# One attention step in another order: products with v behind the scores, and a third of the transposes behind these

## The chip, the cores and the metric

The kernel runs on one core of a Trainium2 chip, as one program. The metric is the device time of one execution in microseconds (us), the median of several. The engines are named as in the profile: PE is TensorE (matmuls and transposes; PEld is its weight load), DVE is VectorE, ACT is ScalarE, POOL is GpSimd, and SP is the engine that issues most DMAs. Each engine works through its own instructions in the order in which the program has them.

## The reference

Three blocks follow each other: attention with a learned position bias, a dense feed-forward block, and an expert block in which each token goes to one of 8 experts. Only the order inside the attention changes.

```
B, H, S, D = 4, 8, 576, 64                              # batch, heads, sequence, head size
scores = q @ k.T / sqrt(D) + bias[head]                 # bias: a small MLP over log distances
attn   = exp(scores - max) / sum                        # softmax over the 576 keys
x      = (attn @ v), heads side by side                 # 2304 tokens x 512
h = x @ w_in ; x = (h - tanh(h)) @ w_out                # dense block, 512 -> 2048 -> 512
out = gate * (relu(x @ w1[e]) @ w2[e]), e = argmax(x @ w_gate)   # 8 experts
```

All arrays are float32.

## The kernel before

The attention is cut into 16 units. A unit is one batch entry and a pair of heads, and it has five steps, one for each block of query rows: blocks 0 to 3 have 128 rows for each of the two heads, and block 4 has the last 64 rows of both heads in one tile. The loop in `emit` (line 431) runs over x = 5 times the unit plus the step and issues what the row of `STEPS` (line 423) for this step names, one after the other. Nothing sorts the instructions afterwards, so this table is the order on every engine. One entry stands for these instructions:

- S0 and S1: the scores of a block and the first half of the softmax. S0 issues the 12 matmuls for both heads (`scores`, line 235; q and k are split in a high and a low part, so three products for each half of the keys; the two heads lie in the two halves of the array's 128 rows). The softmax on DVE (line 267) adds the bias and takes the maximum, once in S0 and once in S1. The scores lie in the two PSUM tiles of the tag `s`.
- E0 and E1: the exponentials on ACT (line 280) of the block of the step before. For block 4, POOL makes a copy (line 284).
- X0, X1 and X2: the transposes of p, the result of the exponentials, two steps later (`p_transposes`, line 311): nine 128 x 128 transposes in three groups of three, each group into one PSUM tile of the tag `xt`, of which there are three. DVE copies the group of X0 out (line 330), ACT the others (line 332). Block 4 has four transposes in X0 (line 335, copied out by ACT in lines 337 and 338) and one in X1 (line 342, copied out in lines 343 and 344).
- V, with a half and a block of keys: products of v with the transposed p (`pv`, line 346), two matmuls for the two heads, in the two halves of the array's columns. Half 0 covers the query blocks 0 and 1 (256 columns), half 1 the blocks 2 to 4 (320 columns). V-03 belongs to the unit before, V00 to this one. After the last block ACT copies the sum out (line 369).
- T and U: transposes of k, of q, or of the last 64 rows of both (`t`), for one or two units ahead (`transposes`, line 193), also into an `xt` tile; ACT copies them out as the high part (line 208). L and M: the low part on DVE (`lows`, line 224, lines 228 and 230), which reads the same PSUM tile once more. Lt ends with a copy on POOL (line 233).
- qk, v, bias, store, store_r: DMA loads and stores on SP. sums and spread: the reciprocals of the softmax sums, and their transpose (line 299).
- `*`: work for the next block that is spread over the attention steps: `Convert.step(x)` (line 499), a conversion of one weight tile every 2.4 steps, in stages: load, then two steps later a scaling on ACT (line 520), a clamp on POOL (line 525), bit operations on DVE (lines 531 to 538), a store; some tiles are split on ACT and DVE instead (lines 639 and 640). Tile i begins at x = 3 + 12 i / 5, rounded down, and is scaled two steps later.

A tile of a tag is given out again in the order in which the program has finished issuing the reads of the tiles before. The next matmul into it waits for the last of these reads. The dense block follows on PE as soon as the attention's instructions have been issued, in the same queues.

Of the kernel before, what the change touches and what calls it, by code (L numbers as in the profile page):

```python
# [127 lines left out]
class Attention:  # L128
# [246 lines left out]
    def begin(self, g):  # L375

        calls = {
            "qk": self.load_qk, "v": self.load_v,
            "bias": lambda i: self.load_bias(0, i),
        }  # L380
        for x, op, i in self.BESIDE:
            if x == g:
                if op in calls:
                    calls[op](i)
                elif op in ("k", "q", "t"):
                    self.transposes(i, op)
                    self.lows(i, op)
                else:
                    self.op(0, i, op)
# [30 lines left out]
    DONE = 3  # L420


    STEPS = (
# [5 lines left out]
    )  # L429

    def emit(self, extra):
# [3 lines left out]
        for x in range(self.DONE, 5 * nu + 5):  # L435
            for op in self.STEPS[x % 5]:
                if op == "*":
# [4 lines left out]
    def op(self, u, i, op):  # L442

        nu = len(self.units)
        x = 5 * u + i
        kind, w = op[0], int(op[-1]) if op[-1].isdigit() else None
        if kind == "S" and u < nu and (i < 4 or w == 0):
            if w == 0:
                self.scores(u, i)
            self.softmax1(u, i, w)  # L450
        elif kind == "E" and 0 <= x - 1 < 5 * nu and ((x - 1) % 5 < 4 or w == 0):
            self.softmax2((x - 1) // 5, (x - 1) % 5, w)
        elif kind == "X" and 0 <= x - 2 < 5 * nu and ((x - 2) % 5 < 4 or w < 2):
            self.p_transposes((x - 2) // 5, (x - 2) % 5, w)
        elif kind in "TU" and u + (1 if kind == "T" else 2) < nu:
            self.transposes(u + (1 if kind == "T" else 2), op[1])
        elif kind in "LM" and u + (1 if kind == "L" else 2) < nu:
            self.lows(u + (1 if kind == "L" else 2), op[1])
        elif kind == "V":
            v = u - 1 if op[1] == "-" else u  # L460
            if 0 <= v < nu:
                self.pv(v, int(op[-2]), (w,))
        elif op in ("sums", "spread", "store", "store_r"):
            if u > 0:
                getattr(self, op)(u - 1)
        elif op == "v":
            if 0 < u < nu - 1:
                self.load_v(u + 1)
        elif op == "qk" and 0 < u < nu - 2:
            self.load_qk(u + 2)  # L470
        elif op == "bias" and u + 1 < nu and self.units[u + 1][0] != self.units[u][0]:
            self.load_bias(self.units[u + 1][0], i)
# [956 lines left out]
```

## Time and profile before

| | us |
|---|---|
| median of 3 runs (lowest, highest) | 1058.62 (1055.51, 1059.51) |
| the profiled execution | 1059.38 |
| its span, first to last instruction | 1057.7 |
| busy in the span: PE, DVE, ACT, POOL | 1012.8, 762.7, 673.0, 186.8 |

The span has four stretches. The bias is made until about 79 us, attention runs until about 375 us, the dense block until about 800 us, and the experts to the end. The steps of the attention that PE runs back to back last from about 106 us on. A PE row of the timeline gives the start of the first matmul of a group and the end of its last; ends are modelled and overlap the next start, so distances between starts are what can be trusted.

### The profile page before, as it was taken

To read this page: it belongs to the slowest core of one execution; us is meant where nothing else is said; L and a number is where in the kernel's file an instruction comes from. 1 tells how busy PE (TensorE), PEld (TensorE's weight loads), DVE (VectorE), ACT (ScalarE), POOL (GpSimd) and SP (SyncE) were. 2 spreads that over 40 slices of the span, in tenths; PEclk is the share of its full clock that TensorE was granted. 3 is DMA by queue.
4 is the path that set the end of the run, shared out by engine and by line. 5 is a ranking of instruction groups with operands and counts; after the bars stand their busy time and mean duration, and the time that the engine had idled before them with its cause. 6 is when DMAs were issued, how large, how long until landed. Compare 5 with 4: busy or idle time off the path is not lost. (4 is left out here: it accounts for less than half of the span.)

```text
span 1057.7 us, 20501 instructions
## 1 busy us (share of the span) xinstructions
PE 1012.8 (96%) x7370; PEld 833.1 (79%) x7370; DVE 762.7 (72%) x1749; ACT 673.0 (64%) x1507; POOL 186.8 (18%) x224
## 2 busy tenths in 40 slices
PE   6788999999999999999999999999999999999994
PEld 3345666666666679889989889898899999999992
DVE  7874788888888789988899889888894544434210
ACT  7775888888878889765665665656883333333211
POOL 1100222222322411010110201202012131222111
PEclk9888999999999999999999999999999999999998
DMA  5747585685674443020200200203124244437200
GB/s 161 233 176 197 139 233 138 151 224 153 175 198 129 152 152 121 1 91 1 67 24 1 91 1 1 90 1 85 53 79 112 86 111 123 124 109 232 76 24 25
DMA packets 113750, 114.67 MB, mean 108 GB/s; under 512 B 67883, under 2 KB 82603, under 8 KB 113644
## 3 DMA queue, kind: packets, MB, share of 16 engines
q1 hardware_dynamic: 109628, 103.26, 34.0%
q0 software_dynamic: 3872, 9.72, 3.1%
q8 instruction: 60, 0.98, 0.4%
q14 instruction: 46, 0.38, 0.1%
q10 hardware_dynamic: 144, 0.33, 0.1%
HBM read 82.36 MB, written 31.18 MB: 107 GB/s over the span
## 5 line engine op out<-in xcount | busy, mean ns | idle before, releaser
L679 PE MATMUL h<-xh,w 128*128 128x384 f32 x768 | 215.4, 341 | 2.2 <-DVE t L698 2.2
L723 PE MATMUL y<-w,gh 128*128 128x512 f32 x576 | 179.4, 393 | 0.0
L679 PEld LDWEIGHTS h<-xh,w 128*128 128x128 f32 x768 | 140.6, 188 | 7.4 <-DVE t L698 3.5
L267 DVE CUSTOM_DVE_ANT_0 p<-s,bias 128x576 f32<-128x576 f32 x144 | 103.7, 753 | 36.7 <-PE s L247 18.8
L679 PE MATMUL h<-xl,w 128*128 128x384 f32 x384 | 129.2, 336 | 0.0
L723 PEld LDWEIGHTS y<-w,gh 128*128 128x128 f32 x576 | 106.6, 188 | 16.0
L1110 PE MATMUL eh<-xh,ew 128*128 128x288 f32 x512 | 117.6, 305 | 0.0
L723 PE MATMUL y<-w,gl 128*128 128x512 f32 x288 | 112.7, 391 | 0.2 <-DVE gl L710 0.2
L1132 PE MATMUL ey<-ehh,ew 128*128 128x288 f32 x512 | 112.7, 296 | 0.0
L280 ACT ACTIVATE p<-p,nm 128x576 f32<-128x576 f32 x144 | 110.7, 771 | 2.2 <-DVE nm L267 2.1
L1120 DVE SCALAR_TENSOR_TENSOR ehl<-eh,ehh 128x288 fp32r<-128x288 f32 x64 | 29.2, 457 | 110.5 <-ACT ehh L1119 101.6
L1119 ACT ACTIVATE ehh<-eh 128x288 fp32r<-128x288 f32 x64 | 26.3, 410 | 125.6 <-PE ey L1132 122.3
L691 ACT ACTIVATE z<-h 128x384 f32<-128x384 f32 x96 | 46.5, 484 | 77.1 <-PE h L679 77.1
L326 PE MATMUL px<-ident,p 128*128 128x128 f32 x576 | 92.8, 285 | 0.1
L358 PE MATMUL pv<-pt,vt 128*64 128x256 f32 (+1 forms) x256 | 87.2, 434 | 2.2 <-ACT pt L337 2.2
L326 PEld LDWEIGHTS px<-ident,p 128*128 128x128 f32 x576 | 63.3, 142 | 31.3 <-ACT p L280 11.1
L359 PE MATMUL pv<-pt,vt 128*64 128x256 f32 (+1 forms) x256 | 87.2, 434 | 0.0
L1110 PEld LDWEIGHTS eh<-xh,ew 128*128 128x128 f32 x512 | 86.6, 190 | 0.3 <-issue 0.2
L1132 PEld LDWEIGHTS ey<-ehh,ew 128*128 128x128 f32 x512 | 85.7, 188 | 0.0
L1110 PE MATMUL eh<-xl,ew 128*128 128x288 f32 x256 | 76.1, 297 | 0.0
L1132 PE MATMUL ey<-ehl,ew 128*128 128x288 f32 x256 | 75.6, 295 | 0.0
L332 ACT ACTIVATE pt<-px 128x384 f32<-128x384 f32 x128 | 60.9, 488 | 20.4 <-PE px L326 19.9
(474 smaller groups left out, 2202.0 us busy)
## 6 DMA issues: line engine op xcount, KB each, us to landing
rw<-in_moe_w SPq DMA_DIRECT2D x64, 256.0 KB
bias_d<-bo SPq DMA_DIRECT2D x36, 320.0 KB
bias<-bias_d SPq DMA_DIRECT2D x16, 576.0 KB
w<-in_moe_w_in SPq DMA_DIRECT2D x16, 512.0 KB
w<-in_moe_w_out SPq DMA_DIRECT2D x16, 512.0 KB
xt_d<-x SPq DMA_DIRECT2D x16, 288.0 KB
w_d<-wc SPq DMA_DIRECT2D x18, 256.0 KB
xf<-xt_d SPq DMA_DIRECT2D x24, 192.0 KB
```

The lines of the kernel that those rows point to most:

```text
L267: nc.vector.tensor_tensor_reduce(st["p"][:, c].rearrange("p (a x) -> p a x", a=2), st["ps", w][:, :, 0:288], bias[:, c].rearrange("p (a x) ...
L280: nc.scalar.activation(p[:, c], p[:, c], AF.Exp, bias=nm[:, w : w + 1], scale=-1.0, accum_out=self.st[u, "sm"][:, x : x + 1])
L326: nc.tensor.transpose(ps[:, 128 * j : 128 * j + 128], p[:, 128 * n : 128 * n + 128], self.ident)
L332: nc.scalar.activation(dst, src, AF.Copy)
L358: nc.tensor.matmul(ps[a, 0:n], v[:, j, :], pt[:, j, 0:n], start=j == 0, stop=False)
L359: nc.tensor.matmul(ps[z, 0:n], v[:, 6 + j, :], pt[:, 5 + j, 0:n], start=j == 0, stop=False)
L679: nc.tensor.matmul(ps[:, 0 : self.N], a, r32(b[:, k, :]), start=k + i == 0, stop=k == 3 and i == 2)
L691: nc.scalar.activation(z, h, AF.Square)
L723: nc.tensor.matmul(self.acc[u, t], r32(a[:, c]), r32(w[:, b, :]), start=m + i == 0, stop=m == 15 and i == 2)
L1110: nc.tensor.matmul(ps[:, 0:SLOT], a, r32(b[:, k, 0:SLOT]), start=k + i == 0, stop=k == 3 and i == 2)
L1120: nc.vector.scalar_tensor_tensor(r32(l), ps[:, 0:SLOT], 0.0, h, op0=ALU.max, op1=ALU.subtract)
L1132: nc.tensor.matmul(st["y", d][:, 0:SLOT], a, r32(b), start=f + i == 0, stop=f == 7 and i == 2)
```

## The change

The five rows of `STEPS` are written anew. The order on PE is now in every step: transposes X0 and X1, the scores, the products with v, the transposes X2, and then those of k or q for a later unit, where the step has them; in step 1, which has no X2, the transposes t stand between X1 and the scores. The scores of a step no longer have transposes directly behind them, and the seven places of a unit at which products with v stand become five. The low parts move about one step later against their transposes: those of k (now Nk) from step 4 into step 0, those of q (Lq) from step 0 into step 1, and those of the last rows (Lt) from step 1 into step 2. `op` now names for all of them the unit after this one. No instruction is added or taken away.

```diff
--- before.py
+++ after.py
@@ -420,12 +420,13 @@
     DONE = 3
 
 
+
     STEPS = (
-        ("X1", "qk", "X0", "S0", "E0", "S1", "E1", "Tq", "X2", "V-03", "Lq", "V-04", "*", "bias"),
-        ("X0", "S0", "E0", "S1", "Tt", "X1", "E1", "X2", "V-10", "Lt", "sums", "*", "bias"),
-        ("X0", "V-11", "E0", "X1", "S0", "X2", "S1", "E1", "V-12", "spread", "*", "v", "bias"),
-        ("X0", "V-13", "E0", "V-14", "X1", "S0", "E1", "X2", "store_r", "S1", "bias", "*"),
-        ("X0", "S0", "V00", "E0", "E1", "X2", "X1", "V02", "V01", "*", "Uk", "Mk", "store", "bias"),
+        ("X0", "Nk", "X1", "qk", "S0", "E0", "S1", "E1", "V-02", "V-03", "X2", "Tq", "*", "bias"),
+        ("X0", "Lq", "X1", "Tt", "S0", "E0", "S1", "E1", "V-04", "sums", "*", "bias"),
+        ("X0", "Lt", "X1", "S0", "E0", "S1", "E1", "V-10", "V-11", "V-12", "X2", "*", "v", "bias"),
+        ("X0", "X1", "S0", "E0", "S1", "E1", "V-13", "V-14", "spread", "X2", "store_r", "bias", "*"),
+        ("X0", "X1", "S0", "E0", "E1", "V00", "V01", "X2", "*", "Uk", "store", "bias"),
     )
 
     def emit(self, extra):
@@ -454,8 +455,9 @@
             self.p_transposes((x - 2) // 5, (x - 2) % 5, w)
         elif kind in "TU" and u + (1 if kind == "T" else 2) < nu:
             self.transposes(u + (1 if kind == "T" else 2), op[1])
-        elif kind in "LM" and u + (1 if kind == "L" else 2) < nu:
-            self.lows(u + (1 if kind == "L" else 2), op[1])
+        elif kind in "LN" and op[1] in "kqt" and 0 <= u and u + 1 < nu:
+            if (u + 1, op[1]) in self.qk:
+                self.lows(u + 1, op[1])
         elif kind == "V":
             v = u - 1 if op[1] == "-" else u
             if 0 <= v < nu:
```

The built programs show what stands on PE and ACT. First PE in the kernel before, in step 1 and at the start of step 2 of a unit: tp8t are the last rows of k and q (t), px_4_1 is X1 of block 4, pv_1 is a block of half 1, px_0_0 and px_0_1 are X0 and X1 of block 0.

```order
L202 MATMUL tp8t<-ident,kn_2623 128x64
L202 MATMUL tp8t<-ident,qn_2627 128x64
L342 MATMUL px_4_1_2974<-ident,p_4_2844 128x128
L358 MATMUL pv_1_2980<-pt_1_2831,vt_108 64x320
L359 MATMUL pv_1_2980<-pt_1_2831,vt_108 64x320
L326 MATMUL px_0_0_2998<-ident,p_0_2912 128x128 x3
L358 MATMUL pv_1_2980<-pt_1_2831,vt_108 64x320
L359 MATMUL pv_1_2980<-pt_1_2831,vt_108 64x320
L326 MATMUL px_0_1_3006<-ident,p_0_2912 128x128 x3
```

Transposes and products with v take turns here, one block at a time.

PE in the changed kernel, from X2 of step 0 to the t transposes of step 1, with the engines that each instruction waits for (an engine's name with _49; DMAHW are DMA queues): px_3_2 is X2, tp8q the transposes of q, px_4_0 and px_4_1 are X0 and X1 of block 4. The scores of step 1 come next.

```order
L326 MATMUL px_3_2_2920<-ident,p_3_2801 128x128 [waits Activation_49]
L326 MATMUL px_3_2_2920<-ident,p_3_2801 128x128 x2
L205 MATMUL tp8q<-ident,qn_2630 128x128 [waits DMAHW1_49,DMAHW0_49,DVE_49]
L205 MATMUL tp8q<-ident,qn_2630 128x128 x3
L335 MATMUL px_4_0_2936<-ident,p_4_2849 128x128 [waits DVE_49,Activation_49]
L335 MATMUL px_4_0_2936<-ident,p_4_2849 128x128 x3
L342 MATMUL px_4_1_2944<-ident,p_4_2849 128x128 [waits Activation_49,Pool_49]
L202 MATMUL tp8t<-ident,kn_2626 128x64 [waits DMAHW7_49,PE_49,Activation_49]
L202 MATMUL tp8t<-ident,qn_2630 128x64 [waits DMAHW2_49]
```

The t transposes have moved from behind the scores to a place in front of them, and all transposes between two visits to v stand together. The wait of tp8t for ACT is one for the second copy out of px_4_0 (line 338): that is the `xt` tile which it gets. Before, it got the tile of px_3_2, a step older.

PE in the changed kernel, the end of step 1 and the start of step 2.

```order
L247 MATMUL s_1_1_2956<-kt_2606,qt_2607 128x288
L361 MATMUL pv_0_2854<-pt_0_2724,vt_108 64x256
L362 MATMUL pv_0_2854<-pt_0_2724,vt_108 64x256
L326 MATMUL px_0_0_2991<-ident,p_0_2910 128x128 x3
L326 MATMUL px_0_1_3000<-ident,p_0_2910 128x128 x3
L247 MATMUL s_2_0_3005<-kt_2606,qt_2607 128x288
```

One block of v follows the scores of step 1, and then come X0 and X1 of step 2 together.

ACT in the kernel before, from the copy of q in step 0 to the second exponential of step 1: p_0 is the block whose exponentials these are.

```order
L208 ACTIVATE qt_2871<-tp8q 128x512
L332 ACTIVATE pt_1_2831<-px_3_2_2924 128x3x128
L369 ACTIVATE x_2934<-pv_0_2847 128x256
L337 ACTIVATE pt_1_2831<-px_4_0_2941 128x4x64
L338 ACTIVATE pt_1_2831<-px_4_0_2941 128x4x64
L280 ACTIVATE p_0_2912,sm_2965<-p_0_2912,nm_0_2913 128x576
L208 ACTIVATE kt_2870<-tp8t 128x64
L208 ACTIVATE qd_106<-tp8t 64x64 x2
L343 ACTIVATE pt_1_2831<-px_4_1_2974 128x64
L344 ACTIVATE tl_2975<-px_4_1_2974 128x64
L280 ACTIVATE p_0_2912,sm_2965<-p_0_2912,nm_0_2913 128x576
```

The first exponential stood right behind the copies of px_4_0.

ACT in the changed kernel, the same place.

```order
L332 ACTIVATE pt_1_2831<-px_3_2_2920 128x3x128
L208 ACTIVATE qt_2869<-tp8q 128x512
L337 ACTIVATE pt_1_2831<-px_4_0_2936 128x4x64
L338 ACTIVATE pt_1_2831<-px_4_0_2936 128x4x64
L343 ACTIVATE pt_1_2831<-px_4_1_2944 128x64
L344 ACTIVATE tl_2945<-px_4_1_2944 128x64
L208 ACTIVATE kt_2868<-tp8t 128x64
L208 ACTIVATE qd_106<-tp8t 64x64 x2
L280 ACTIVATE p_0_2910,sm_2972<-p_0_2910,nm_0_2911 128x576 x2
L369 ACTIVATE x_2978<-pv_0_2854 128x256
```

Both exponentials of block 0 now stand behind all copies of px_4 and of the t transposes. On SP the order is the same word for word; on POOL the copy of line 233 has moved behind one conversion clamp in six of the units.

## Rows read from the trace of the kernel before

**Rows 1.** Busy time by stretch; a stretch is one unit (us, share after it).
```profile
core 0: us, PE busy (x) PEld busy (x) DVE busy (x) ACT busy (x) POOL busy (x), PEclk, DMA share, GB/s
...
206.57:224.72 18.15, 18.10 (x150) 12.11 (x149) 14.88 (x38) 15.29 (x41) 4.58 (x4) 1.00 0.76 208
...
sum 201.25, PE 199.91 PEld 133.53 DVE 165.45 ACT 168.48 POOL 51.89; mean PE 18.17 PEld 12.14 DVE 15.04 ACT 15.32 POOL 4.72
```

**Rows 2.** Busy time by stretch: the first steps, and the end of attention.
```profile
79.00:106.00 27.00, 21.78 (x163) 13.83 (x151) 11.37 (x31) 15.45 (x40) 2.45 (x3) 0.87 0.76 198
350.00:400.00 50.00, 47.29 (x308) 36.00 (x307) 40.88 (x86) 41.55 (x97) 11.66 (x12) 1.00 0.45 143
```

**Rows 3.** Timeline of PE, one unit: start, us, line, operation, tiles, count.
```profile
208.50 0.66 PE L335 MATMUL px<-ident,p 128*128 128x128 f32 x4
...
211.14 0.55 PE L326 MATMUL px<-ident,p 128*128 128x128 f32 x3
211.62 0.48 PE L358 MATMUL pv<-pt,vt 128*64 128x320 f32 x1
...
212.31 0.55 PE L326 MATMUL px<-ident,p 128*128 128x128 f32 x3
212.78 1.05 PE L247 MATMUL s<-kt,qt 64*128 64x288 f32 x12
...
218.17 0.87 PE L326 MATMUL px<-ident,p 128*128 128x128 f32 x6
219.09 1.07 PE L247 MATMUL s<-kt,qd 128*128 128x288 f32 x6
220.09 0.43 PE L358 MATMUL pv<-pt,vt 128*64 128x256 f32 x1
...
220.67 0.88 PE L326 MATMUL px<-ident,p 128*128 128x128 f32 x6
221.48 0.43 PE L358 MATMUL pv<-pt,vt 128*64 128x256 f32 x1
...
222.49 0.66 PE L205 MATMUL tp9k<-ident,kn 128*128 128x128 f32 x4
```

**Rows 4.** Timeline of ACT in the same unit, columns as above.
```profile
207.26 0.60 ACT L208 ACTIVATE qt<-tp8q 128x512 fp32r<-128x512 f32 x1 [0.43 <-PE tp8q L205]
207.75 0.48 ACT L332 ACTIVATE pt<-px 128x384 f32<-128x384 f32 x1
...
209.19 0.39 ACT L337 ACTIVATE pt<-px 128x256 f32<-128x256 f32 x1 [0.19 <-PE px L335]
209.47 0.38 ACT L338 ACTIVATE pt<-px 128x256 f32<-128x256 f32 x1
...
210.49 0.22 ACT L208 ACTIVATE kt<-tp8t 128x64 fp32r<-128x64 f32 x1
...
211.07 0.22 ACT L343 ACTIVATE pt<-px 128x64 f32<-128x64 f32 x1
...
211.29 0.78 ACT L280 ACTIVATE p<-p,nm 128x576 f32<-128x576 f32 x1
211.96 0.20 ACT L280 ACTIVATION_READ_ACCUMULATOR p<-p,nm 128x1 f32 x1
...
219.14 0.67 ACT L520 ACTIVATE wc<-w 128x512 f32<-128x512 f32 x1
219.71 0.76 ACT L280 ACTIVATE p<-p,nm 128x576 f32<-128x576 f32 x1
...
220.47 0.76 ACT L280 ACTIVATE p<-p,nm 128x576 f32<-128x576 f32 x1
```

**Rows 5.** Timeline of DVE, a softmax of step 2 in the same unit.
```profile
213.87 0.76 DVE L267 CUSTOM_DVE_ANT_0 p<-s,bias 128x576 f32<-128x576 f32 x1 [0.16 <-PE s L247]
...
215.23 0.08 DVE L267 DVE_READ_ACCUMULATOR2_ANT nm<- 128x1 f32 x1
```

**Rows 6.** Timeline of DVE in the first attention steps.
```profile
84.51 0.76 DVE L267 CUSTOM_DVE_ANT_0 p<-s,bias 128x576 f32<-128x576 f32 x1 [3.44 <-DMA bias<-bias_d]
```

## The prediction

> **What bounds the kernel now.** I read the busy shares by stretch first, then PE's timeline over one unit, then ACT's at the place where the new order puts PE and ACT behind each other. Eleven units in a row, each cut from the start of one group of q transposes (Tq) to the next, take 201.25 us together, 18.30 each, and PE is busy in 199.91 of them; the unit that I look at takes 18.15, with PE busy 18.10, DVE 14.88 and ACT 15.29 [rows 1]. So PE sets the pace and almost never waits. But a PE that is always busy is not a PE that does only work. The starts in its timeline show that [rows 3]. A group of three transposes takes 0.48 from its start to the start of the products with v behind it (211.14 to 211.62), a group of six takes 0.81 (220.67 to 221.48): three transposes are worth 0.33 (0.11 each), and the group costs 0.15 beside its work. A block of v (256 columns) takes 0.58 (220.09 to 220.67), two in a row take 1.01 (221.48 to 222.49): a block is 0.43, and the group again costs 0.15 beside it. A change of the array's shape (128 x 128 for transposes, two halves of rows for the scores of blocks 0 to 3, two halves of columns for v) costs about 0.15 per visit.
>
> Of this busy share alone one would say that there is nothing to win, 0.05 us in the unit. The Trainium skill (Perfetto Trace Analysis, Identifying the Most-Contended Engine) says that busy time of matmuls is a bad measure of PE's headroom and that the busy share of weight loads is a better one; here that is 12.11 of 18.15 [rows 1], which leaves up to 6 us in a unit. The starts above agree with the page.
>
> **What the change takes away.** Counting the visits over a unit of PE's order: before, 22 (t behind the scores of step 1 and the scores of block 4 behind transposes are no change of shape); after, 14. Transposes are visited 5 times instead of 11, v 5 times instead of 7, scores in row halves 4 times as before, which makes 8 visits less: 8 x 0.15 = 1.2 us per unit. All matmuls stay, so their work stays.
>
> One wait goes as well. Six transposes are 0.66, yet the scores of block 4 start 0.92 after the six before them (218.17 to 219.09) [rows 3]; they wait 0.26 for DVE, whose softmax is through 2.53 after the start of the scores before (212.78 [rows 3] to 215.31, the end of the second row of [rows 5]). In the new order two blocks of v, the spread, X2, X0 and X1 lie between the two groups of scores, over 3 us. Saved: 1.2 + 0.26 = 1.46 per unit.
>
> One kind of change has no row before: scores in row halves directly followed by v in column halves, four times per unit. From full-width scores to v it costs what every change costs (219.09 to 220.09 is 1.00 for six matmuls). I take 0.15 in all, as in the count of visits. The bounds are nothing (as t behind the scores) and 0.30 (the two changes that stood here before): 0.6 per unit to either side. The Trainium skill (TensorEngine Tiling (Array Packing), Overview, Key Properties) says that a change of tiling mode drains the engine; by that rule the lower bound falls away. No run here shows it yet.
>
> **What the change adds: a wait in step 1.** The t transposes now stand in front of the scores of step 1 and get the tile that X0 of the same step has just filled, so they wait for ACT's second copy out of it. Behind them on PE stand the scores of step 1, V-04, and X0 and X1 of step 2. I count from the first transpose of Tq. ACT's first copy starts 0.69 after the start of four transposes (208.50 in [rows 3], 209.19 in [rows 4]), so the copy of q starts at 0.69, and ACT takes the next one 0.49 later (207.26, 207.75), at 1.18. This is the first copy of px_4_0; the second follows 0.28 later, at 1.46, and ends 0.38 after that, at 1.84 [rows 4]. PE would be ready for t at 1.09 (Tq 0.44, X0 0.44, X1 0.11, a change 0.10). It starts at about 1.88: 0.79 lost.
>
> The loss grows at the exponentials of step 0, which ACT now has behind all of these copies. t is done and its three copies start at about 2.15, they take 0.58 (210.49 to 211.07), the first exponential starts at 2.73 and the second 0.76 later (219.71, 220.47), at 3.49. It is there for PE 0.87 after its start (211.29 to the end of the read at 212.16), at 4.36 [rows 4]. PE after t: scores from 2.03, v from 3.03, X0 of step 2 from 3.61, just when the first exponential is done (3.60). X1 would have its second transpose, the first that reads the second head, at 4.10 and gets it at 4.40: 0.30 more. Together 1.1 us per unit, for the units 1 to 14 that prepare another. The scores of step 2 then start 2.7 after those of step 1, and DVE needs 2.53: this cover is thin, and each tenth that DVE is later costs a tenth.
>
> When a conversion is scaled in step 0, the scaling stands on ACT between the copy of q and px_4_0 and takes 0.57 (219.14 to 219.71) [rows 4]. By the rule that tile i is scaled at x = 5 + 12 i / 5, that is so at x = 5, 45, 50, 55, 60, 65, the units 1 and 9 to 13. There the loss is 1.67.
>
> What else moves costs nothing. SP issues the same DMAs in the same order. The low parts on DVE stay ahead of their readers: Nk, Lq and Lt are read in the next unit, and Lq frees its tile for X1 of step 2, over 2 us later. POOL's copy of kt is behind one clamp at times, with three steps to spare. DVE and ACT, at 14.88 and 15.29 per unit [rows 1], still fit into 17.8.
>
> **The sum.** A plain unit: -1.46 + 1.1 = about -0.37. With a scaling in step 0: -1.46 + 1.67 = +0.2. Units 2 to 8 and 14 are plain: 8 x -0.37 = -3.0. Units 9 to 13: +1.0. Unit 15 prepares no other and has only the wait for the exponentials, some 0.4: -1.0. Units 0 and 1 wait for DMAs of the bias and the first weights (DVE sat idle for 3.44 there [rows 6]): nothing. Total -3.0. The profiled execution took 1059.38, 0.76 above the median of 1058.62: 1056.4 by its own time, 1055.6 by the median. I forecast 1056.
>
> **The rivals.** What a measurement of this kernel can tell from no change is about 0.5%, 5.3 us.
>
> A, slower: the copy of px_4_0 comes late on ACT. ACT has two copies, Tq's and the exponential of block 4 to do in step 0 and over 4 us of work in step 1. If X2's copy and leftovers of the conversion still stand ahead in every unit, the loss at t is 0.57 longer in the 8 plain units too (+4.6) and by one copy, 0.49, in all 13 (+6.4): 1056 + 11 = 1067. It decides from the point where a unit loses more than 1.46. For it: ACT has 15.29 of 18.15 filled, and its order is strict. Against: before Tq's copy ACT sat idle for 0.43 [rows 4].
>
> B, the waits are half as long, because the copies begin sooner than their rows before say, where ACT came from other work: 13 x -0.55 = -7: 1049. For it: three of the latencies are read off starts at which ACT had just finished something. Against: each step of the chain is a dependence in the program.
>
> C, the unseen change from scores to v costs the full 0.30, of which one in four hides in the wait: 13 x 0.45 = +6: 1062.
>
> D, the change does not do what it says: fewer visits, but each unit waits elsewhere for what it gains, because ACT and DVE with their orders need some 18.2 anyhow. Then nothing changes: 1059.
>
> E, the clock. In the first steps, with PE busy in 21.78 of 27 us, the granted clock was 0.87, so part of it ran at 1.2 GHz instead of 2.4; at the end of attention, with 47.29 of 50 and a gap of over 2 us, it stayed at 1.00 [rows 2]. The new order is busy for 16.7 of 17.8, the same share as the latter. If the clock fell to 0.87 all the same, a quarter of the time would run at half speed, 2.4 us per unit: 1090.
>
> **Chances and range.** Forecast 0.50 (its own range 1052 to 1061), A 0.13, B 0.17, C 0.10, D 0.07, E 0.03. Faster by over 0.5% (below 1053.3) are B and a small part of the forecast's range, 0.25. Slower by over 0.5% (above 1063.9) are A, E and an edge of C, 0.16. The rest, 0.59, is no change. From 1047.5 to 1064 the range leaves out most of A, E and the low end of B, and holds both bounds of the unseen change (13 x 0.6 = 8 to either side).
>
> **What would show it.** In the profile after: units of 17.7 to 17.9 from Tq to Tq, and of 18.3 to 18.5 for units 9 to 13; the first of t about 0.8 behind px_4_1 and waiting for line 338 on ACT; X1 of step 2 waiting some 0.3 for the exponential; scores of block 4 without a wait; v starting about 0.22 after the last scores. The forecast is wrong if plain units take 18.3 or more (A or D, told apart by where PE sits idle), or less than 17.3 (B), if scores to v takes 0.35 (C), or if the granted clock is below 1.00 (E).

## The result, and the profile after

| | before | after |
|---|---|---|
| median, us (lowest to highest) | 1057.07 (1053.72 to 1059.51) | 1068.04 (1065.19 to 1070.01) |
| the profiled execution; its span | 1059.38; 1057.7 | 1065.19; 1063.4 |
| busy PE, DVE, ACT, POOL | 1012.8, 762.7, 673.0, 186.8 | 1000.5, 757.7, 674.0, 186.9 |

The changed kernel is slower: 1.0104 times the time before, 95% interval 1.0061 to 1.0147. I had forecast 1056, with 1064 as the upper end. Six later executions give 1068.24 and 1.0098 (1.0072 to 1.0124). PE is busy for 12.3 us less and the whole takes longer. The two profiled executions are only 5.8 us apart, since that of the changed kernel is the fastest of its four; the places below account for these 5.8.

Two distances on PE divide the attention: the 12 units 2 to 13, from the first transpose of tp3q to that of tp15q, and the end, from there to the last product with v. Before they take 219.52 and 40.04, after 222.67 and 43.73; ahead of them after is 1.18 shorter (the profiles of all versions differ by up to 4.6 there), and the dense block and the experts keep the distance that they begin with. So the units lost 3.15 where I had forecast a gain of some 1.6, and the end lost 3.69 where I had forecast a gain of 1.4.

The windows answer to [rows 1] and the second of [rows 2]: units 3, 7 and 12, a piece of unit 12, the end.

```profile
core 0: us, PE busy (x) PEld busy (x) DVE busy (x) ACT busy (x) POOL busy (x), PEclk, DMA share, GB/s
132.20:150.15 17.95, 17.04 (x151) 12.23 (x150) 14.48 (x38) 15.32 (x40) 4.31 (x5) 1.00 0.85 244
204.97:223.21 18.24, 17.24 (x150) 12.20 (x149) 14.61 (x38) 15.52 (x40) 4.42 (x4) 1.00 0.83 222
297.61:318.63 21.02, 18.55 (x150) 13.14 (x149) 15.30 (x38) 15.48 (x40) 4.35 (x4) 0.92 0.71 188
304.00:307.00 3.00, 3.00 (x19) 2.09 (x20) 2.42 (x8) 2.39 (x6) 0.29 (x1) 0.50 1.13 280
350.00:400.00 50.00, 43.16 (x293) 32.51 (x292) 36.74 (x79) 37.76 (x90) 10.99 (x12) 0.97 0.50 156
```

Unit 3 takes 17.95 (18.24 before) and unit 7 18.24 (18.15 before). PE is now idle for 0.9 to 1.0 in these units; in unit 7 that was 0.05 before. Unit 12 takes 21.02, and in a part of it, as at the end of attention, the granted clock is 0.50, the level of 1.2 GHz.

PE's timeline of unit 7 answers to [rows 3] (start, duration, line, operation, count, and in brackets the idle time with what ended it).

```profile
204.97 0.60 PE L205 MATMUL tp8q<-ident,qn 128*128 128x128 f32 x4
205.41 0.60 PE L335 MATMUL px<-ident,p 128*128 128x128 f32 x4
205.85 0.27 PE L342 MATMUL px<-ident,p 128*128 128x128 f32 x1
206.81 0.27 PE L202 MATMUL tp8t<-ident,kn 64*128 64x64 f32 x1 [0.69 <-ACT pt L338]
...
207.92 0.43 PE L361 MATMUL pv<-pt,vt 128*64 128x256 f32 x1
...
208.68 1.20 PE L326 MATMUL px<-ident,p 128*128 128x128 f32 x6
209.81 1.06 PE L247 MATMUL s<-kt,qt 64*128 64x288 f32 x12
...
216.03 1.46 PE L326 MATMUL px<-ident,p 128*128 128x128 f32 x9
217.24 1.03 PE L247 MATMUL s<-kt,qd 128*128 128x288 f32 x6
```

What I had counted on is there. t starts 1.84 after the first of Tq (206.81 - 204.97; forecast 1.88) and waits for line 338. Block 0's X0 and X1 start 0.76 after the block of v, where 0.58 was due, and take 1.13 to the scores, where six transposes and a change took 0.81 [rows 3]: the wait for the exponentials, 0.18 and 0.32. Nothing waits at the scores of block 4. What I had not counted on is the last two rows: nine transposes take 1.21 (216.03 to 217.24), while those of other units take 0.90 (197.58 to 198.48 in unit 6).

ACT at the same place, which answers to [rows 4]:

```profile
205.18 0.49 ACT L332 ACTIVATE pt<-px 128x384 f32<-128x384 f32 x1 [1.24 <-PE px L326]
205.61 0.60 ACT L208 ACTIVATE qt<-tp8q 128x512 fp32r<-128x512 f32 x1
206.10 0.38 ACT L337 ACTIVATE pt<-px 128x256 f32<-128x256 f32 x1
206.37 0.39 ACT L338 ACTIVATE pt<-px 128x256 f32<-128x256 f32 x1
...
207.18 0.22 ACT L208 ACTIVATE kt<-tp8t 128x64 fp32r<-128x64 f32 x1 [0.19 <-PE tp8t L202]
...
207.76 0.77 ACT L280 ACTIVATE p<-p,nm 128x576 f32<-128x576 f32 x1
...
208.54 0.76 ACT L280 ACTIVATE p<-p,nm 128x576 f32<-128x576 f32 x1
```

The copies follow each other as forecast: px_4_0 at 1.13 and 1.40 after Tq (forecast 1.18 and 1.46), the exponentials at 2.79 and 3.57 (2.73 and 3.49).

Then the places that the forecast did not have. First DVE in step 3 and 4 of the same unit:

```profile
215.26 0.75 DVE L267 CUSTOM_DVE_ANT_0 p<-s,bias 128x576 f32<-128x576 f32 x1
...
215.94 0.76 DVE L267 CUSTOM_DVE_ANT_0 p<-s,bias 128x576 f32<-128x576 f32 x1
...
216.61 0.27 DVE L301 COPY rt<-rp 9x128 f32<-9x128 f32 x1
```

The spread takes one of the three `xt` tiles, and in unit 7 X1 of step 4 gets it next. Its copy (line 301) stands behind both halves of a softmax; with the spread in step 2 it is done long before that. The nine transposes take 0.31 and 0.32 longer in units 7 and 8 by their starts, the time that X1 waits for this copy. In units 9 to 11 they take 0.47, 0.48 and 0.74 longer, 2.3 in all, but there X1 does not get the spread's tile. Unit 9:

```profile
253.25 0.49 ACT L332 ACTIVATE pt<-px 128x384 f32<-128x384 f32 x1
```
```profile
252.55 0.55 DVE L330 COPY pt<-px 128x384 f32<-128x384 f32 x1
...
254.37 0.27 DVE L301 COPY rt<-rp 9x128 f32<-9x128 f32 x1
```

Here X0 starts at 253.25, 0.15 after the end of DVE's line 330, and X1 at 253.80, 0.06 after the end of ACT's line 332, while line 301 has not begun. By the built program X0 gets the tile of X0 of step 3 and X1 that of X2: which tile a transpose gets is not always what the order of the entries says. The spread holds the third tile all the while; that it is the reason for these waits too is likely, not shown.

A smaller place has nothing to do with the spread: in units 4 to 6 X0 of step 0 starts 0.24, 0.22 and 0.52 late, behind DVE's copy of X0 of step 4 (line 330), 1.0 in all. These delays are the same in versions 1, 3, 4, 7 and 8 below.

Second, unit 12, on ACT (the first row is from the kernel before) and then on PE:

```profile
300.72 0.67 ACT L520 ACTIVATE wc<-w 128x512 f32<-128x512 f32 x1 [0.45 <-DMA w<-in_moe_w_in]
```
```profile
300.07 0.67 ACT L522 ACTIVATE wc<-w 128x512 f32<-128x512 f32 x1 [1.23 <-DMA w<-in_moe_w_in]
300.65 0.37 ACT L337 ACTIVATE pt<-px 128x256 f32<-128x256 f32 x1
...
301.95 0.77 ACT L280 ACTIVATE p<-p,nm 128x576 f32<-128x576 f32 x1
```
```profile
302.87 1.24 PE L326 MATMUL px<-ident,p 128*128 128x128 f32 x6 [1.50 <-ACT p L280]
304.04 1.81 PE L247 MATMUL s<-kt,qt 64*128 64x288 f32 x12
305.78 0.79 PE L358 MATMUL pv<-pt,vt 128*64 128x320 f32 x1
```

The scaling of a conversion (line 522) waits 1.23 for its load, and the copies of px_4_0, the copies of t and the exponentials stand behind it on ACT. PE sits idle for 1.50, and then the clock falls: the 12 scores take 1.74 from start to the next start (304.04 to 305.78) instead of 0.99, and the v behind them 2.50 instead of 1.77. Unit 12 takes 2.86 more than unit 13. Two things meet here. SP issued that load at 294.10, directly behind store_r and a bias load; before, at 293.30, in a unit that began 0.21 later. And ACT comes to the scaling 1.23 after the first of Tq, before 2.45 after it. The load itself is not later: ACT's waits end at 300.07 now and at 300.72 before.

Third, the end, on POOL, on PE, and on SP, first in the kernel before:

```profile
370.49 0.70 POOL L284 COPY p<-p 128x64 f32<-128x64 f32 x1
```
```profile
371.25 0.33 PE L342 MATMUL px<-ident,p 128*128 128x128 f32 x1 [0.32 <-POOL p L284]
```
```profile
361.09 0.63 SPq L308 DMA_DIRECT2D r_d<-rt  x1
```

Then in the changed kernel:

```profile
371.83 0.99 POOL L661 TENSOR_TENSOR xf<-xf,xr 128x384 f32<-128x384 f32 x1 [4.13 <-DMA xr<-r_d]
373.54 1.28 POOL L661 TENSOR_TENSOR xf<-xf,xr 128x384 f32<-128x384 f32 x1 [0.71 <-DMA xr<-r_d]
374.77 0.23 POOL L284 COPY p<-p 128x64 f32<-128x64 f32 x1
```
```profile
370.97 0.66 PE L335 MATMUL px<-ident,p 128*128 128x128 f32 x4 [0.54 <-ACT p L280]
375.05 0.33 PE L342 MATMUL px<-ident,p 128*128 128x128 f32 x1 [3.43 <-POOL p L284]
...
376.72 0.79 PE L358 MATMUL pv<-pt,vt 128*64 128x320 f32 x1 [0.50 <-ACT x L369]
```
```profile
365.37 0.64 SPq L308 DMA_DIRECT2D r_d<-rt  x1
```

The products of the dense block's first x with the reciprocals (line 661) stand on POOL ahead of the last copy of p (line 284). They wait for r_d to be read back, and the DMA that writes r_d is issued at 365.37, 4.28 later than before; the copy of p comes 4.28 later as well. Of these 4.28 the scores of step 1 in this unit bring 1.06 along (355.80 against 354.74), and the place of the spread 3.2. X1 of block 4 waits 3.43 for that copy, where it waited 0.32, and v and the dense block wait behind it; then the clock falls again.

### The profile page after: what moved, and what is told of

Same layout as the page of the kernel before. It is cut to its first block, busy times and chain, and to the rows that moved or that the text cites. A ratio compares the mean times of both kernels' runs of the same rounds, so it can differ in the third digit from the quotient of the medians.

```text
span 1063.4 us, 20482 instructions
## 1 busy us (share of the span) xinstructions
PE 1000.5 (94%) x7370; PEld 836.3 (79%) x7370; DVE 757.7 (71%) x1749; ACT 674.0 (63%) x1507; POOL 186.9 (18%) x224
## 5 line engine op out<-in xcount | busy, mean ns | idle before, releaser
L326 PE MATMUL px<-ident,p 128*128 128x128 f32 x576 | 88.5, 284 | 5.8 <-ACT p L280 1.5
L358 PE MATMUL pv<-pt,vt 128*64 128x256 f32 (+1 forms) x256 | 78.3, 430 | 0.5 <-ACT x L369 0.5
L359 PE MATMUL pv<-pt,vt 128*64 128x256 f32 (+1 forms) x256 | 78.3, 430 | 0.0
L247 PE MATMUL s<-kt,qt 64*128 64x288 f32 x768 | 73.4, 316 | 4.4 <-ACT bo L106 4.0
```

The lines of the kernel that those rows point to most:

```text
L247: nc.tensor.matmul(ps[w][:, c, 0:288], r32(q[r, a, 128 * i : 128 * i + 128] if i < 4 else self.qd[u % 2][:, a, :]), r32(k[r, b, kc : kc + ...
L326: nc.tensor.transpose(ps[:, 128 * j : 128 * j + 128], p[:, 128 * n : 128 * n + 128], self.ident)
L358: nc.tensor.matmul(ps[a, 0:n], v[:, j, :], pt[:, j, 0:n], start=j == 0, stop=False)
L359: nc.tensor.matmul(ps[z, 0:n], v[:, 6 + j, :], pt[:, 5 + j, 0:n], start=j == 0, stop=False)
```

## The experiments

Each row is a version of the changed kernel, or of the kernel before where it says so. The kernel before was timed beside each (medians 1057.5 to 1058.6). "Units" and "end" are the two distances above in the profiled execution, against the kernel before.

| | median, us | against before, 95% | units | end |
|---|---|---|---|---|
| changed, as it is (6 executions more) | 1068.24 | 1.0098 (1.0072 to 1.0124) | +3.30 | +5.42 |
| 1, spread back in step 2 | 1060.67 | 1.0025 (1.0011 to 1.0040) | +1.26 | +1.45 |
| 2, Tt behind the scores | 1070.20 | 1.0126 (1.0100 to 1.0151) | +3.85 | +5.41 |
| 3, Tt behind the exponentials | 1057.55 | 1.0003 (0.9987 to 1.0020) | -5.64 | +2.89 |
| 4, both 1 and 3 | 1052.70 | 0.9951 (0.9930 to 0.9971) | -7.15 | -0.79 |
| 5, before, V-11 moved | 1064.38 | 1.0075 (1.0055 to 1.0094) | +4.10 | +0.07 |
| 6, before, spread late | 1062.80 | 1.0057 (1.0035 to 1.0079) | -0.82 | +5.45 |
| 7, 4 with `*` earlier | 1051.19 | 0.9948 (0.9929 to 0.9966) | -7.53 | -0.68 |
| 8, 7 with E0 first | 1054.48 | 0.9968 (0.9949 to 0.9986) | -7.81 | +1.57 |
| 9, last copy of p on DVE | 1062.41 | 1.0045 (1.0027 to 1.0063) | +3.24 | +0.14 |

**1. The spread.**

```diff
 step 2: ... "V-10", "V-11", "V-12", 
+        "spread", 
         "X2", ...
 step 3: ... "V-13", "V-14", 
-        "spread", 
         "X2", "store_r", ...
```

> The changed kernel with one entry put back: spread stands in step 2 again, behind V-12, and no longer at the end of step 3. Theory: the late spread costs most of what the change lost. The reciprocals reach DRAM some 4.3 us earlier, so the last copy of p on POOL is no longer behind multiplications that wait for them (3.4 us less at the end of attention); X1 of step 4 no longer waits for DVE's copy of the spread tile (0.3 to 0.7 in units 8 to 12, 2.3 in all); the load of the weight that ACT waits for in unit 12 comes about 0.8 earlier. Together 6 to 8 us less than the changed kernel, 1060 to 1062 us. Rival: these places were late because each unit is, and lose their time elsewhere: 1066 to 1068, as the changed kernel.

1060.67, as the theory had it: 7.6 less than the changed kernel. The write of r_d is issued at 359.47, and POOL's last copy of p starts at 368.95; PE waits 0.6 for it. In unit 12 ACT no longer waits for the load (line 522 runs from 298.23, right behind the copy of q), and the unit takes 18.70. The load is now issued 4.9 before the first of Tq, in the changed kernel 3.5. The units with longer transposes in step 4 are 7 to 11; the expectation counts them one too high, and puts all their time to the spread's copy. Part of the time in the units comes back: the transposes of step 3 take 0.2 longer in units 2 to 6 and 0.4 in units 12 and 13, and in units 9 to 11 the scores of block 4 wait 0.3 to 0.4 for DVE. So units 7 to 11 gain 1.1 in all, not 2.3, and unit 12 gains 2.3.

**6. The same entry moved in the kernel before**, the other way.

```diff
-("X0", "V-11", "E0", "X1", "S0", "X2", "S1", "E1", "V-12", "spread", "*", "v", "bias"),
-("X0", "V-13", "E0", "V-14", "X1", "S0", "E1", "X2", "store_r", "S1", "bias", "*"),
+("X0", "V-11", "E0", "X1", "S0", "X2", "S1", "E1", "V-12", "*", "v", "bias"),
+("X0", "V-13", "E0", "V-14", "X1", "S0", "E1", "X2", "spread", "store_r", "S1", "bias", "*"),
```

> The kernel before with one entry moved: spread stands in step 3 behind X2, right in front of store_r, and no longer in step 2. Theory: the late spread alone costs time, whatever else the order is: the last copy of p on POOL comes some 3 us later behind the multiplications that wait for the reciprocals, and transposes behind the spread tile wait for DVE in part of the units: 3 to 6 us more, 1061 to 1064 us. Rival: only in the changed order are ACT, DVE and SP late enough for it to matter: 1057 to 1059.

```profile
367.00 0.66 PE L335 MATMUL px<-ident,p 128*128 128x128 f32 x4
371.86 0.47 PE L342 MATMUL px<-ident,p 128*128 128x128 f32 x1 [4.21 <-POOL p L284]
372.27 0.80 PE L358 MATMUL pv<-pt,vt 128*64 128x320 f32 x1
```

5.35 us more, all of it at the end: PE waits 4.21 at the same instruction, and the clock is down behind it (the first v takes 0.80). The units lose nothing here, so the half of the expectation on transposes behind the spread tile fails for this order.

**9. The end alone.** In the last unit the copy of p goes to DVE.

```diff
-nc.gpsimd.tensor_copy(p[:, 576:640], p[:, 512:576])
+(nc.vector if u == len(self.units) - 1 else nc.gpsimd).tensor_copy(p[:, 576:640], p[:, 512:576])
```

> The changed kernel, with the copy of p of the last block (line 284) on DVE instead of POOL in the last unit alone, so that it no longer stands behind the multiplications that wait for the late reciprocals. Theory: of the three places at which the late spread costs, this takes away the largest, 3.4 us of wait at the end of attention, and the half-speed stretch of the clock that followed it there: 3 to 5 us less than the changed kernel, and less than half the distance to the kernel before stays. Rival: PE then waits at the next place for the same multiplications (the dense block's x), and only 0 to 1 us is gained.

```profile
371.93 0.66 PE L335 MATMUL px<-ident,p 128*128 128x128 f32 x4 [0.55 <-ACT p L280]
...
375.26 0.48 PE L358 MATMUL pv<-pt,vt 128*64 128x320 f32 x1 [1.99 <-ACT x L369]
```

5.8 us less than the changed kernel. A second wait for the same late reciprocals comes up behind it (1.99 for ACT's line 369, in front of which ACT splits the x that POOL multiplies), but no clock drop follows within the end of attention, and the end takes 40.18, as before. So the end is the largest of the three places.

**2 and 3. The wait at t.**

```diff
-("X0", "Lq", "X1", "Tt", "S0", "E0", "S1", "E1", "V-04", "sums", "*", "bias"),
+("X0", "Lq", "X1", "S0", "Tt", "E0", "S1", "E1", "V-04", "sums", "*", "bias"),    # 2
+("X0", "Lq", "X1", "S0", "E0", "S1", "E1", "Tt", "V-04", "sums", "*", "bias"),    # 3
```

> The changed kernel with Tt behind the scores of step 1 (X0, Lq, X1, S0, Tt, E0, ...), so that the t transposes wait beside the scores' work; the exponentials stand behind the copies of t on ACT, as in the changed kernel. Theory: the wait at t (0.81 per unit) goes, but PE then stands at X0 and X1 of step 2 for the exponentials, which come as late as before: 0 to 0.2 less per unit, 1065 to 1068 us. Rival: the wait at t is time lost on its own, 0.8 for 13 units: 1057 to 1059.

> The changed kernel with Tt behind the scores and behind both exponentials of step 1 (X0, Lq, X1, S0, E0, S1, E1, Tt, V-04, ...). Theory: the chain copies of px_4, t, copies of t, exponentials, X1 of step 2 was what ate the saved changes of shape; with the exponentials ahead of t's copies both waits (0.81 and 0.45 per unit) go but for some 0.3 at X1: 0.9 to 1.0 less per unit, 12 to 13 us in 13 units, 1055 to 1057 us. Rival: ACT and DVE with their orders need some 18.1 per unit anyhow, and the wait turns up elsewhere: 1064 to 1068.

Version 2 gains nothing (1070.20; 1065 to 1068 were expected). t no longer waits, it follows the scores, and X0 of step 2 then waits for the exponential instead:

```profile
207.12 0.21 PE L202 MATMUL tp8t<-ident,kn 64*128 64x64 f32 x1
...
208.94 1.20 PE L326 MATMUL px<-ident,p 128*128 128x128 f32 x6 [0.96 <-ACT p L280]
```

Version 3 takes 10.7 us off, near the 12 to 13 expected: units 2 to 8 take 17.0 to 17.6. X0 and X1 of step 1 lead to the scores in 0.64, where it took 1.40 from them to t: the wait at t was 0.76. Of the wait at X0 and X1 of step 2 some 0.3 stay, as expected (1.12 from X0 to the scores). In units 9 to 11 the gain is 0.6 instead of 0.9, because there the exponentials stand behind a scaling.

**4, 7 and 8. Both edits, and further.** Version 7 is version 4 with `"*"` of step 0 in front of `"X2", "Tq"`; version 8 is 7 with `"E0"` of step 1 in front of `"X0"`.

> Both edits: spread in step 2, and Tt behind the scores and the exponentials of step 1. If each theory holds, the gains add: 18 to 20 us less than the changed kernel, 1048 to 1050 us, less than the kernel before. If ACT and DVE bound the unit at 18.1, only the end of attention gains: 1060 to 1062.

> The version with both edits (spread in step 2; Tt behind the scores and exponentials of step 1), and the conversion (*) of step 0 in front of X2 and Tq, where ACT stood idle for 1.2 us. Theory: in units 9 to 13 the scaling no longer delays the copies of q and px_4_0 and the exponentials behind them; X0 of step 2 waited 0.46 longer there than in the other units: 2 us less than that version, 1050 to 1051 us. Rival: the scaling waits for its DMA at the earlier place and delays the copy of X2: 1053 or more.

> The version before this one, with the first exponential of step 1 in front of the copies of px_4 as well (E0, X0, Lq, X1, S0, S1, E1, Tt, ...). Theory: X0 of step 2 still waited 0.35 per unit for the exponentials; with E0 ahead of four copies (0.8 on ACT) that wait goes but for 0.1: 3 to 4 us less again, 1046 to 1048 us. Rival: the copies of px_4, and with them the tiles that t and X0 get, are later by 0.76 and PE waits for these: no gain, 1050 to 1052 us.

Version 4 beats the kernel before by 0.5%. Its unit 8:

```profile
222.63:239.66 17.03, 16.93 (x150) 12.32 (x149) 14.57 (x38) 15.15 (x40) 4.32 (x4) 1.00 0.86 213
```

PE is busy in 16.93 of 17.03. It is 3 us short of the expectation. By units and end the two gains do add: against the changed kernel again, versions 1 and 3 gain 6.0 and 11.5 there and version 4 16.7. The rest lies outside these two distances, and its cause is open. In units 9 to 13 the scaling on ACT still costs 0.46 each. Version 7 takes that away (17.34 where 4 has 17.87 in unit 9) but in unit 12 the load is late again and now holds X2's copy, with 1.40 on PE. It lies 1.5 under version 4, within what the two intervals leave open. Version 8 (1054.48; 1046 to 1048 were expected) gains 0.3 in the units and loses 2.2 at the end, where PE waits 1.24 for the last copy of p and the clock falls; why that copy is late is open. In the units the second exponential, not the first, is the late one, because the four copies now stand between the two.

```profile
206.31 0.77 ACT L280 ACTIVATE p<-p,nm 128x576 f32<-128x576 f32 x1
...
207.06 0.37 ACT L337 ACTIVATE pt<-px 128x256 f32<-128x256 f32 x1
...
207.80 0.80 ACT L280 ACTIVATE p<-p,nm 128x576 f32<-128x576 f32 x1
```

**5. Changes of shape alone.**

```diff
-("X0", "V-11", "E0", "X1", "S0", "X2", "S1", "E1", "V-12", "spread", "*", "v", "bias"),
+("X0", "E0", "X1", "S0", "X2", "S1", "E1", "V-11", "V-12", "spread", "*", "v", "bias"),
```

> The kernel before with one block of v moved in step 2: V-11 stands beside V-12, behind X2, and no longer between X0 and X1. This takes away two changes of the array's shape per unit and nothing else. Theory (0.15 per change): 0.3 less per unit, 4 to 5 us in 15 units, 1053 to 1055 us, if X1 doesn't then wait for the second exponential of step 1. Rival: a change of shape costs nothing by itself, the gaps between starts are waits: 1058.

Slower by 6.9 us, and the price of a change holds all the same. Units 2 to 6 take 18.58, 0.33 more than before. X1 now waits for the exponential, here in unit 7 (18.47, before 18.15):

```profile
213.24 0.66 PE L326 MATMUL px<-ident,p 128*128 128x128 f32 x4
214.30 0.44 PE L326 MATMUL px<-ident,p 128*128 128x128 f32 x2 [0.40 <-ACT p L280]
```

From the fourth transpose's start to the fifth's it is 0.73 instead of 0.11, 0.62 of wait; 18.58 - 0.62 is 17.96, 0.29 under 18.25. The two changes gave 0.3, and the block of v had covered 0.6 of wait.

**The changed kernel again.**

> The changed kernel as it is, a second profile and more times beside the other. Theory: its executions differ by how many half-speed stretches of TensorE's clock they have (0.8 us for each 0.001 of the mean granted clock), and it has more of them than the kernel before (0.979 against 0.985): 1066 to 1070 us, a mean clock of 0.977 to 0.981, and the waits at t, X1 of step 4, unit 12 and the end of attention as in the first profile. Rival: the first four times were a chance draw, and it lies within 0.5% of the kernel before: 1059 to 1063.

1068.24, with the same waits (3.5 at the end, 1.76 in unit 12), inside the theory's bounds. The mean granted clock of the executions of the changed kernel is 0.979, that of the kernel before 0.985. Within one kernel an execution is 0.7 us longer for each 0.001 less (the 16 of the kernel before in this comparison: 1062.8 at 0.978, 1054.5 at 0.991). By that, 4 of the 10 us between the medians go with the clock. They seem to belong to the spread: with the spread back (version 1) the mean clock is 0.985 again, and with the late spread in the old order (version 6) it is 0.981, where the kernel before has 0.986 beside it.

## Why the prediction was wrong

**Changes of shape: right.** Unit 3 without its waits (0.76 at t, 0.50 at X0 and X1) takes 16.69. Before, its scores of block 4 waited 0.37 by the prediction's way of counting (0.26 is unit 7), and without that it takes 17.87: 1.18 for 8 visits, forecast 1.2.

```profile
145.17 0.87 PE L326 MATMUL px<-ident,p 128*128 128x128 f32 x6
146.20 1.05 PE L247 MATMUL s<-kt,qd 128*128 128x288 f32 x6 [0.16 <-DVE nm L267]
```

Experiment 5 finds the same 0.15. The change that had no row, scores to v, has one now: 0.22 from the last score's start to v (256 columns), as from full-width scores before. That is the value taken; rival C is out. The Trainium skill (TensorEngine Tiling (Array Packing), Tiling Modes, Key Properties) says that the array drains at a change of tiling mode, and the lower bound of nothing does fall away.

**The wait in step 1: right, one term too small.** 0.76 for 0.79 at t; 0.50 for 0.30 at X0 and X1. A unit with no other wait gains 0.29 (unit 3), forecast 0.37. Experiment 3 shows that this chain, and no bound of ACT or DVE, set the 18 us: with the exponentials ahead units 3 to 5 take 17.0 to 17.3, so rival D falls. Rival B falls too, the waits are not shorter. Rival A's 1067 lies near the time by chance: the copy of px_4_0 was to come late, and it starts at 1.13, forecast 1.18.

**Scalings in step 0: wrong in mechanism, too high.** In units 9 to 13 t waits 0.94, not 1.36. The built program gives t another tile there, that of Tq, whose last reader is DVE's line 230: in unit 9 t starts at 243.47, 0.06 after that line ends and 0.32 before line 338 does.

**"What else moves costs nothing": this step failed.** In the profiled execution the units 2 to 13 lose 6.2 at places that the sum did not have: 1.0 in units 4 to 6, 2.3 at the transposes of step 4 in units 7 to 11, 2.9 in unit 12. Without these they would have gained 3.0, where 1.6 were forecast. The end is 3.7 longer, where 1.4 less was forecast. Most of this is the spread. It is one small transpose, and I counted it only as filling between two groups of scores. It is moved from step 2 to the end of step 3, and three things hang on it: the `xt` tile that it holds (the wait of X1 for its copy, 0.6 in units 7 and 8), store_r and what stands behind it on SP (the load of unit 12, for which ACT also asks 1.2 earlier), and the reciprocals that POOL waits for ahead of the last copy of p (3.4). I wrote that SP issues the same DMAs in the same order. It does, and store_r among them waits some 3 us longer for its data, with the others behind it. Experiment 1 gets back 7.6 of the 10 us, experiment 6 makes the kernel before 5.35 slower with this entry alone. Version 1 is still 2.4 us over the kernel before: the 1.0 in units 4 to 6 stays in it, and so do waits for DVE in units 9 to 11.

**The clock: rival E at the wrong place.** I asked whether the whole stretch would be busy enough, and [rows 2] had a gap of over 2 us with the clock at 1.00. What came instead are single gaps with half speed behind them: the wait of over 3 us at the end is followed by it in all five profiles that have it (changed, again, 2, 3 and 6), the 1.5 to 2.4 in unit 12 in all five that have that (changed, again, 2, 3 and 9). It is no rule: gaps of 1.2 and 1.4 in unit 12 of versions 8 and 7 had none behind them, and two of the seven profiles without the long wait (1 and 8) show half speed near the end too. The gap of [rows 2], 2.2 us at the start of the dense block, is in all twelve profiles; nine show half speed behind it, the kernel before, the changed one's first profile and version 7 do not. Which gap does it is open; that 4 us of the difference go with the clock rests on the times' slope, and no run held the clock fixed.

## What to carry to other kernels

When a step is moved, follow what it hands out as well as where it stands: its tile to the next transposes, its DMA to everything queued behind it, and its data to the last reader, which may be another block's work in front of an instruction that this block needs. A wait on PE that moves when its instruction moves is another engine's order; move the work on that engine, not the waiting one. What stands between two dependent groups may cost time by itself and still be cover worth twice as much.

## What was not expected of the hardware

The scores of block 4 start 0.03 after the start of the last transpose before them, and t's scores 0.01 after t's first transpose; so where the shape stays, the start of the next group follows without the 0.09 that I had read off behind transposes of other shapes. Half speed behind a single gap can cost as much again as the gap: in unit 12 the gap is 1.50 and the half speed 1.48 (0.75 in the scores, 0.73 in v). At the end of attention it is less: behind the gap of 3.43 four blocks of v take 0.53 to 0.59 each instead of 0.27 to 0.32, 1.1 in all.
